# A dynamic convolution feeding a maxout layer: the start's sums, one unit's transpose and the last stores rearranged

## The chip, the core and the metric

The kernel runs on one core of a Trainium2 chip. The metric is device time in microseconds (us), from the start of the program to its end; lower is better. Times of whole runs are medians over several runs. A profile is one execution, and its span runs from the first instruction recorded to the last.

The engines are named as in the profile: PE is TensorE (PEld its weight loads), DVE is VectorE, ACT is ScalarE, POOL is GpSimd, SP is SyncE. Each works through its own queue in order.

## What is computed

```python
# x [8, 4160, 192], weight_gen [8, 4160, 8 heads, 7 taps]
w   = softmax(weight_gen, axis=-1)                     # over the 7 taps
y[b, s, h*24+g] = sum_k w[b, s, h, k] * x_pad[b, s + k, h*24+g]   # causal: x_pad has 6 zero rows ahead
# then, on y as [33280, 192], with w1, w2 [192, 1024] and w_out [1024, 192]
out = maximum(y @ w1, y @ w2) @ w_out
```

Inputs and output are float32; the kernel works in bfloat16 where it multiplies.

## The kernel before

**Layout.** The 33280 rows are laid over 128 partitions, 260 consecutive rows ("columns" in the code) to each. Columns come in batches of 16 (16 batches, and a 17th of 4). A batch is cut into pieces and a piece gives a unit: batches 0 and 1 have four pieces of 4 columns each (units 0 to 7), later ones two of 8 (units 8 to 35), and the last is unit 36 with 4. TensorE's unit of work is a tile, one per column, 260 in all: a tile is one 128-wide chunk of the 1024 hidden features for 8 columns, or two chunks for 4 columns.

**The convolution.** For a batch, `exp_sum` (L127, ACT) takes the exponentials, `red` (L132, DVE) sums them over the taps, `ln` (L135, ACT) takes the logarithm, `shift` (L140, DVE) subtracts it from the raw weights, and `weights` (L148, ACT) takes the exponential again, which is the softmax, written twice over in bfloat16. `mul` (L157, DVE) multiplies all seven taps of a piece into `m_t`. `adds` sums the taps in three instructions: L172 (taps 3, 4, 5 onto 0, 1, 2, which leaves the four slices 0, 1, 2 and 6), L177 and L179 (into `y_t`); with `first=True` only L172 is issued.

**Transposing.** From unit 8 on, `transpose` (L188) moves `y_t` through the DMA crossbar, issued on SP; a small copy on POOL, the gate (L194), waits for it, and the next loads of `x` and `weight_gen`, issued on POOL too, stand behind that gate. Units 0 to 7 go through `sum_transpose` (L215) instead: TensorE multiplies slices of `m_t` with an identity and so sums the remaining taps and transposes at once, into PSUM; ACT copies the result out (L220). Units 0 to 3 have all seven taps summed on TensorE, units 4 to 7 four of them.

**The maxout.** Since max(h1, h2) = h1 + relu(h2 - h1), `hid_tile` (L247, PE) multiplies with the difference w2 - w1 (`wd`), `relu` (L257, ACT) clips it, and the output is y (w1 w_out) (L299, in `out_first`) plus the clipped part times w_out (L287), both into PSUM. `evac` (L343, ACT) copies results to `o_t` and issues the stores on ACT (L353). The small product w1 w_out (`w10`) is made at the start: `w1_transposed` (L542) transposes w1 on TensorE in 16 pieces, eight of 128 rows and eight of 64, ACT copies them to `w1t` (L548), `w10_product` (L587) multiplies.

**Order.** The schedule is written out by hand: each engine runs its instructions in the order in which the code issues them. Tiles are worked in groups: eight of two tiles (tiles 0 to 15), then groups of three, and a last one of one tile. `hidden(g, now, between, beside)` issues for a group the hidden matmuls of all tiles but the last, the first part of the results of the columns `now` (`out_first`), relus, the last tile, then the second part of the results and their evacuation. ACT relays a signal between the two parts (`relay`, L320). `extra(t)` issues the convolution of later batches: two pieces per 16 tiles, with `red`, `shift`, `ln`, `exp_sum` and `weights` of the batches after them between. Groups 0 to 3 and what lies around them are written line by line (L551 to L614); `rest_of_1` and `early` (L620 to L636) do so for groups 4 to 7.

**Buffers.** In groups 0 to 7 PSUM has two hidden tiles (`hd`) and two of tag `op`, which results, sum-transposes, w1's transposes and the w10 product share. After that there are "ab" for the first two tiles of a group, "c" for the third and a single one, "r", for results. `rest_of_results` (L426) finishes the last 8 columns in three parts, in "r", "ab" and "c". There are two buffers each for `xb_t`, `en_t` and `y_t`, and six for `yt`.

Of the kernel before, what the change touches and what calls it, by code (L numbers as in the profile page):

```python
# [17 lines left out]
def _sub(base: bass.AP, off: int, dims):  # L18
    ap = [list(base.ap[0])] + [[int(s), int(c)] for s, c in dims]
    return dataclasses.replace(base, offset=base.offset + off, ap=ap)  # L20
# [3 lines left out]
def kernel(  # L24
# [9 lines left out]
    nc = tc.nc  # L34
# [90 lines left out]
    def exp_sum(b):  # L125
        e_ts[b] = pe_.tile([P, BATCHES[b][1] * WGC], FP32, name="e_t", tag="e")
        nc.scalar.activation(out=e_ts[b], in_=wg_ts[b], func=AF.Exp)  # L127

    def red(b):
        TH = BATCHES[b][1] * H  # L130
        s_ts[b] = psm.tile([P, TH], FP32, name="sum_t", tag="sum")
        nc.vector.reduce_sum(out=s_ts[b], in_=_sub(e_ts.pop(b), 0, [[K, TH], [1, K]]), axis=AX.X)  # L132

    def ln(b):
        nc.scalar.activation(out=s_ts[b], in_=s_ts[b], func=AF.Ln)  # L135
# [7 lines left out]
    def weights(b, o):  # L143

        N = dict(pieces(b))[o] * H
        if b not in en_ts:
            en_ts[b] = pen.tile([P, 16 * WGC * 2], BF16, name="en_t", tag="en")
        nc.scalar.activation(  # L148
            out=_sub(en_ts[b], o * WGC * 2, [[2 * N, K], [2, N], [1, 2]]),
            in_=_sub(wg_ts[b], o * WGC, [[1, K], [K, N], [0, 2]]), func=AF.Exp,  # L150
        )


    def mul(b, o):

        n = dict(pieces(b))[o]
        nc.vector.tensor_tensor(  # L157
            out=m_t[:, K * o * D:K * (o + n) * D],
            in0=_sub(xb_ts[b], o * D, [[D, K], [1, n * D]]),
            in1=_sub(en_ts[b], o * WGC * 2, [[2, K * n * H], [0, G // 2], [1, 2]]),  # L160
            op=ALU.mult,
        )
# [40 lines left out]
    def half(j):  # L203
        return slice(64 * j, 64 * j + 64)

    def sum_transpose(u, taps=range(K)):

        b, o, n = UNITS[u]
        nb = n // 2 * 3
        yps = ps["r" if "r" in ps else "o"].tile([P, 1024], FP32, name="yps", tag="op")  # L210
        for k in range(nb):
            for t in taps:
                for j in range(2):
                    at = (K * o + t * n + k // 3 + j * n // 2) * D + k % 3 * 64
                    nc.tensor.matmul(  # L215
                        yps[half(j), k * P:(k + 1) * P], lhsT=m_t[:, at:at + 64],
                        rhs=ident, start=(t == taps[0]), stop=(t == taps[-1]), skip_group_check=True,
                    )
        yt = pyt.tile([P, 8 // 2 * 3 * P], BF16, name="yt", tag="yt")
        nc.scalar.copy(out=yt[:, 0:nb * P], in_=yps[:, 0:nb * P])  # L220
        yt_ts[u] = yt
# [46 lines left out]
    def place(p):  # L268

        u, i, _ = column(2 * p)  # L270
        b, o, n = UNITS[u]
        return BATCHES[b][0] + o + i, n // 2
# [36 lines left out]
    def out_second(now, go):  # L309

        for c in now[::2]:
            for f in range(FCH):
                for j in range(2):
                    mm = out_hidden(c + 1 - j, f, j)
                    if c == now[0] and f == 0:
                        tc.add_manual_dep(mm.ins, go.ins.name, SYNC, reason="bank of the other half")
# [8 lines left out]
    def evac(p, n):  # L325

        tile_, at = op_at[p]
        o = o_t[0]
        if p == NT // 2 - 1:

            for j, copy, eng in ((0, nc.scalar.copy, nc.scalar), (1, nc.vector.tensor_copy, nc.sync)):
                c = place(p)[0] + 2 * j
                copy(out=o[:, c % 24 * D:(c % 24 + 1) * D], in_=tile_[:, at + j * 512:at + j * 512 + D])  # L333
                eng.dma_start(
                    out=bass.AP(tensor=out.tensor, offset=c * D, ap=[[CPP * D, P], [1, D]]),
                    in_=o[:, c % 24 * D:(c % 24 + 1) * D],
                )
            return
        runs = [[q for q in range(p, p + n) if column(2 * q)[0] == u]
                for u in range(column(2 * p)[0], column(2 * (p + n - 1))[0] + 1)]  # L340
        for qs in runs:
            c, h = place(qs[0])
            nc.scalar.copy(out=_sub(o, c % 24 * D, [[D, len(qs)], [h * D, 2], [1, D]]),  # L343
                           in_=_sub(tile_, at + (qs[0] - p) * D, [[D, len(qs)], [512, 2], [1, D]]))
        stores = []
        for q in range(p, p + n):
            u, i, _ = column(2 * q)
            if u < NU - 1 and i == UNITS[u][2] // 2 - 1:
                stores.append((place(q)[0] - i, 2 * (i + 1)))
            if u == NU - 1:  # L350
                stores.extend((place(q)[0] + 2 * j, 1) for j in range(2))
        for c, w in stores:
            nc.scalar.dma_start(  # L353
                out=bass.AP(tensor=out.tensor, offset=c * D, ap=[[CPP * D, P], [1, w * D]]),
                in_=o_t[0][:, c % 24 * D:(c % 24 + w) * D],
            )


# [32 lines left out]
    def out_room(now, tag=None):  # L391
        tag = tag or ("r" if "r" in ps else "o")
        w, name = {"ab": (2048, "ab"), "c": (1024, "c")}.get(tag, (1024, "op"))
        tile_ = ps[tag].tile([P, w], FP32, name="op_ps", tag=name)
        for c in now:
            op_at[c // 2] = tile_, (c - now[0]) // 2 * D

    def hidden(g, now=(), between=lambda: None, beside=lambda: None):


        t0, n = GROUPS[g]
        rd = room(g)
        for t in range(t0, t0 + n - 1):
            hid_tile(t)
        if now:
            out_room(now)
            last = out_first(now)
        if len(now) > 2:
            relu(rd, t0, n - 1)
        else:  # L410
            for t in range(t0, t0 + n - 1):
                relu(rd, t, 1)
        if now:
            go = relay(last)
        hid_tile(t0 + n - 1)
        if len(now) > 2:
            beside()
        relu(rd, t0 + n - 1, 1)
        between()
        if now:  # L420
            out_second(now, go)
            evac(now[0] // 2, len(now) // 2)
        if len(now) <= 2:
            beside()
# [25 lines left out]
    with tc.tile_pool(name="pstage", bufs=1) as pstage:  # L450
# [85 lines left out]
        def w1_transposed():  # L536

            tp = ps["o"].tile([P, 1024], FP32, name="tp", tag="op")[:, :].bitcast(BF16)
            for fi in range(FCH):
                o = fi // 4 * 1024 + fi % 4 * D  # L540
                for at, kind, nr in ((0, "E", P), (P, "T", 64)):
                    nc.tensor.matmul(  # L542
                        tp[:, o + at:o + at + nr],
                        lhsT=w1[kind][0:nr, fi * P:(fi + 1) * P],
                        rhs=ident[0:nr, 0:nr], is_transpose=True, skip_group_check=True,
                    )
            for h in range(2):
                nc.scalar.copy(out=w1t[:, 4 * h * D:4 * (h + 1) * D],  # L548
                               in_=tp[:, h * 1024:h * 1024 + 4 * D])

        warm = ps["h"].tile([P, 1024], FP32, name="warm", tag="hd")  # L551

# [15 lines left out]
        nc.scalar.copy(out=w1["T"], in_=ws["T", 0])  # L568
        w_diff(1, nc.vector.tensor_copy)
        mul(0, 8)  # L570
        sum_transpose(1)
        exp_sum(1)
        red(1)
# [1 line left out]
        ln(1)  # L575
        shift(1)
        mul(0, 12)
        w1_transposed()
        weights(1, 0)
        weights(1, 4)  # L580

        def w10_product():

# [13 lines left out]


        hidden(2)
        mul(1, 0)  # L600
        adds(1, 0, True)
        exp_sum(2)
        sum_transpose(2)
        load_x(2, 0, 16)
        load_wg(4, nc.gpsimd)
        red(2)
        mul(1, 4)
        adds(1, 4, True)
        hidden(3)
        w10_product()  # L610
        sum_transpose(3)
        weights(1, 8)
        weights(1, 12)
        ln(2)  # L614

    pout = ctx.enter_context(tc.tile_pool(name="pout", bufs=1))
    o_t.append(pout.tile([P, 24 * D], FP32, name="o_t", tag="o"))
# [2 lines left out]
    def rest_of_1():  # L620
        mul(1, 8)
        shift(2)
        adds(1, 8, True)
        mul(1, 12)
        red(3)
        adds(1, 12, True)


    none = lambda: None
    early = {  # L630
        3: (none, lambda: (exp_sum(3), rest_of_1())),
        4: (lambda: sum_transpose(4, (0, 1, 2, K - 1)), lambda: weights(2, 0)),
        5: (lambda: sum_transpose(5, (0, 1, 2, K - 1)), none),
        6: (lambda: (weights(2, 8), ln(3), sum_transpose(6, (0, 1, 2, K - 1))), lambda: load_x(3, 0, 8)),
        7: (lambda: sum_transpose(7, (0, 1, 2, K - 1)), none),
    }  # L636

    def extra(t):
# [29 lines left out]
    out_room(OUTS[3])  # L668
    go = relay(out_first(OUTS[3]))
    out_second(OUTS[3], go)  # L670
    evac(OUTS[3][0] // 2, len(OUTS[3]) // 2)
    early[3][1]()
    for g in range(4, len(GROUPS)):
# [40 lines left out]
```

## Time and profile before

| what | value |
|---|---|
| median of 11 runs | 423.01 us (421.83 to 425.58) |
| the profiled execution's own time | 422.35 us |
| its span | 420.6 us |
| PE, DVE, ACT, POOL busy | 405.1, 376.9, 359.9, 72.4 us |
| granted TensorE clock | 0.998 |
| from a unit's `mul` to that of the unit two later (a batch of 16 columns) | 23.84 us |
| PE: 16 transposes of w1 (L542) | 1.8 us for eight of 128 rows, 1.6 us for eight of 64, by the records |
| PE: one 128-column sum-transpose matmul (L215) | 220 ns on record, 48 of them start within 1.37 us |
| DVE: L172, L177, L179 of a 4-column piece | 1355, 959 and 558 ns |
| ACT: copy of a sum-transpose (L220) | 802 ns |

A row of the timeline gives the start in us from the start of the span, the duration, the engine, the line, the operation, out<-in by the program's names, shapes, and in brackets the idle time of the engine before it with what ended it. A row of the groups ends with busy time, the mean duration in ns and the idle time before. Matmul records overlap, since matmuls are pipelined: the distance between starts is what one costs in a stream. An engine name with a q (ACTq, SPq) is the issue of a DMA.

### The profile page before, as it was taken

The numbers are of one execution on the slowest core, as the hardware profiler recorded it, in microseconds if no ns is written. First come the engines' busy times: TensorE is split into PE (matmuls) and PEld (weight loads), VectorE is DVE, ScalarE is ACT, GpSimd is POOL, SyncE is SP. The second block draws the span as 40 slices with busy tenths as digits, with TensorE's granted clock in tenths as the row PEclk, the third lists the DMA queues.
The fourth block names the chain that finished last, engine by engine and source line by source line (L and its number), as shares of the span: only waits on it lengthen the run. The fifth ranks groups of instructions, "written<-read, shape, count | busy, mean of one in ns | idle before, by whom it ended". The sixth has DMA issues, their size and how long they took to land.

```text
span 420.6 us, 15949 instructions
## 1 busy us (share of the span) xinstructions
PE 405.1 (96%) x7405; PEld 327.7 (78%) x7405; DVE 376.9 (90%) x176; ACT 359.9 (86%) x416; POOL 72.4 (17%) x102
## 2 busy tenths in 40 slices
PE   7899999999999999999999999999999999999984
PEld 7789899777777777777787777777787777877784
DVE  5999999998999999999999999999999999996000
ACT  5897889999998989898999899898999899887851
POOL 1510101211220121222201212201203221310000
PEclk9999999999999999999999999999999999999999
DMA  8975547686568776865786767777795786556113
GB/s 243 258 173 151 107 66 197 151 156 95 185 139 182 196 154 168 197 165 146 181 173 125 187 151 195 179 116 195 179 187 129 125 220 99 119 157 134 77 78 115
DMA packets 60259, 65.70 MB, mean 156 GB/s; under 512 B 47617, under 2 KB 48513, under 8 KB 60192
## 3 DMA queue, kind: packets, MB, share of 16 engines
q0 software_dynamic: 8128, 24.11, 28.1%
q1 hardware_dynamic: 46448, 15.10, 21.9%
q10 hardware_dynamic: 5616, 25.46, 15.7%
q8 instruction: 58, 0.95, 0.9%
q14 instruction: 9, 0.07, 0.1%
HBM read 35.96 MB, written 25.56 MB: 146 GB/s over the span
## 4 chain that ended last, share of the span: by engine, by line
DVE 68%; PE 20%; ACT 6%; issue 3%; DMA 1%; ACTq 1%; DVEq 0%
DVE m_t L157 35%; DVE m_t L172 14%; DVE m_t L177 9%; PE op_ps L287 8%; PE hd L247 7%; ACT rd_t L257 3%; DVE sum_t L132 3%; DVE wg_t L140 3%; DVE y_t L179 3%; PE op_ps L299 2%; PE yps L215 1%; ACT o_t L343 1%; DMA wg_t<-in_weight_gen_dram 1%; PE hdp L247 1%; ACT en_t L148 1%
## 5 line engine op out<-in xcount | busy, mean ns | idle before, releaser
L257 ACT ACTIVATE rd_t<-hd 128x1024 bf16<-128x1024 f32 (+1 forms) x206 | 234.6, 1184 | 31.7 <-PE hd L247 31.3
L287 PE MATMUL op_ps<-wo,rd_t 64*128 64x192 bf16 x4160 | 210.4, 243 | 0.1
L287 PEld LDWEIGHTS <-rd_t 64*128 64x128 bf16 x4160 | 180.3, 94 | 16.1 <-ACTq L320 0.3
L247 PE MATMUL hd<-yt,wd 64*128 64x512 bf16 (+1 forms) x1584 | 187.5, 360 | 0.9 <-ACT rd_t L257 0.9
L157 DVE TENSOR_TENSOR m_t<-xb_t,en_t 128x10752 bf16<-128x10752 bf16 (+1 forms) x37 | 187.5, 5070 | 0.2 <-ACT en_t L148 0.2
L247 PEld LDWEIGHTS <-wd 64*128 64x128 bf16 x1776 | 93.2, 94 | 42.2 <-issue 2.4
L194 POOL CAST gate<-yt 128x1 f32<-128x1 bf16 x29 | 36.4, 1257 | 280.8 <-DMA yt<-y_t 280.8
L172 DVE TENSOR_TENSOR m_t<-m_t 128x4608 bf16<-128x4608 bf16 (+1 forms) x33 | 78.2, 2369 | 0.1
L343 ACT COPY o_t<-op_ps 128x384 f32<-128x384 f32 (+1 forms) x99 | 57.1, 587 | 10.9 <-PE op_ps L287 10.8
L299 PE MATMUL op_ps<-w,yt 64*128 64x192 bf16 x780 | 55.4, 243 | 4.4 <-ACT o_t L343 4.3
L299 PEld LDWEIGHTS <-yt 64*128 64x128 bf16 x780 | 38.5, 94 | 21.7 <-issue 6.7
L177 DVE TENSOR_TENSOR m_t<-m_t 128x3072 bf16<-128x3072 bf16 (+1 forms) x29 | 50.2, 1730 | 1.0
L148 ACT ACTIVATE en_t<-wg_t 128x896 bf16<-128x896 f32 (+1 forms) x37 | 34.1, 936 | 1.9 <-ACT o_t L343 0.8
L333 DVE COPY o_t<-op_ps 128x192 f32<-128x192 f32 x1 | 0.4, 358 | 31.4 <-ACT o_t L333 31.4
L179 DVE TENSOR_TENSOR y_t<-m_t 128x1536 bf16<-128x1536 bf16 (+1 forms) x29 | 27.4, 944 | 1.0
L115 POOL DMA_DIRECT2D xb_t<-in_x_dram x32 | 17.2, 539 | 23.7 <-DVE m_t L157 15.7
L132 DVE TENSOR_REDUCE sum_t<-e_t 128x128 f32<-128x896 f32 (+1 forms) x17 | 17.6, 1038 | 3.0 <-ACT e_t L127 3.0
L140 DVE TENSOR_TENSOR wg_t<-wg_t,sum_t 128x896 f32<-128x896 f32 (+1 forms) x17 | 17.8, 1045 | 2.4 <-ACT sum_t L135 2.4
L127 ACT ACTIVATE e_t<-wg_t 128x896 f32<-128x896 f32 (+1 forms) x17 | 15.8, 930 | 3.9 <-DMA wg_t<-in_weight_gen_dram 3.0
L215 PE MATMUL yps<-ident,m_t 128*64 128x128 bf16 x528 | 16.5, 220 | 1.3 <-DVE m_t L157 1.3
L215 PEld LDWEIGHTS <-m_t 128*64 128x64 bf16 x528 | 15.2, 110 | 2.8 <-DVE m_t L157 1.5
L257 ACT ACTIVATE rd_t<-hdp 128x1024 bf16<-128x1024 f32 x16 | 15.8, 1032 | 1.2 <-PE hdp L247 1.2
(45 smaller groups left out, 86.8 us busy)
## 6 DMA issues: line engine op xcount, KB each, us to landing
out_dram<-o_t ACTq DMA_DIRECT2D x28, 768.0 KB, 4.5
xb_t<-in_x_dram POOLq DMA_DIRECT2D x28, 384.0 KB, 5.1
wg_t<-in_weight_gen_dram POOLq DMA_DIRECT2D x14, 448.0 KB, 6.5
xb_t<-xb_t POOLq DMA_DIRECT2D x16, 288.0 KB, 5.3
out_dram<-o_t ACTq DMA_DIRECT2D x8, 384.0 KB, 3.1
wg_t<-in_weight_gen_dram SPq DMA_DIRECT2D x2, 448.0 KB, 5.3
xs<-in_x_dram SPq DMA_DIRECT2D x2, 384.0 KB, 6.6
xb_t<-in_x_dram POOLq DMA_DIRECT2D x1, 768.0 KB, 8.0
```

Of the source, the lines that this page charges most:

```text
L148: nc.scalar.activation(out=_sub(en_ts[b], o * WGC * 2, [[2 * N, K], [2, N], [1, 2]]), in_=_sub(wg_ts[b], o * WGC, [[1, K], [K, N], [0, 2]] ...
L157: nc.vector.tensor_tensor(out=m_t[:, K * o * D:K * (o + n) * D], in0=_sub(xb_ts[b], o * D, [[D, K], [1, n * D]]), in1=_sub(en_ts[b], o * W ...
L172: nc.vector.tensor_tensor(out=taps(0, 1, 3), in0=taps(0, 1, 3), in1=taps(3, 1, 3), op=ALU.add)
L177: nc.vector.tensor_tensor(out=taps(0, 2, 2), in0=taps(0, 2, 2), in1=taps(1, 5, 2), op=ALU.add)
L179: nc.vector.tensor_tensor(out=_sub(y_ts[b], o * D, [[64, 2], [P, 3 * w // 2], [1, 64]]), in0=taps(0, 1, 1), in1=taps(2, 1, 1), op=ALU.add,)
L194: nc.gpsimd.tensor_copy(out=gate, in_=yt[:, 0:1])
L215: nc.tensor.matmul(yps[half(j), k * P:(k + 1) * P], lhsT=m_t[:, at:at + 64], rhs=ident, start=(t == taps[0]), stop=(t == taps[-1]), skip_g ...
L247: nc.tensor.matmul(hid_out(t, f, j), lhsT=wd[half(j), s * F + f * P:s * F + (f + 1) * P], rhs=_sub(yt_ts[u][half(j), :], (s + j) % 3 * P, ...
L257: nc.scalar.activation(out=rd[:, k * 1024:(k + n) * 1024], in_=hd[:, at:at + n * 1024], func=AF.Relu)
L287: return nc.tensor.matmul(op_out(c), lhsT=rd[half(r), k * 1024 + at:k * 1024 + at + P], rhs=wo[half(r), f * D:(f + 1) * D], start=False, s ...
L299: nc.tensor.matmul(op_out(c + j), lhsT=yt_ts[u][half(j), (3 * i + (s + j) % 3) * P:(3 * i + (s + j) % 3 + 1) * P], rhs=w10[half(j), s * D: ...
L343: nc.scalar.copy(out=_sub(o, c % 24 * D, [[D, len(qs)], [h * D, 2], [1, D]]), in_=_sub(tile_, at + (qs[0] - p) * D, [[D, len(qs)], [512, 2 ...
```

## The change

Five things are rearranged; the arithmetic stays the same.

- `w1_transposed` issues the eight pieces of 128 rows first and then the eight of 64, and no longer copies the result: the two copies to `w1t`, and `weights(1, 0)` and `weights(1, 4)` after them, are issued behind `hidden(2)`.
- Columns 8 to 11 (unit 2): L172 is issued on VectorE behind `mul(0, 8)`, ahead of `red(1)`, and the sum-transpose takes four taps in place of seven.
- Softmax steps move: `exp_sum(2)` and `red(2)` behind `w10_product` and `mul(1, 4)`; `ln(2)` behind the second part of the first results; `exp_sum(3)` and `red(3)` behind group 4, ahead of `weights(2, 0)`.
- Columns 28 to 31 (unit 7): all three adds are issued on VectorE (behind `red(3)`), and `transpose(7)` moves the result through the crossbar, issued behind group 6, in place of the sum-transpose in group 7. Its gate on POOL comes ahead of `load_x(3, 0, 8)`.
- The last results: the group of a single tile, the last one, writes its results to "ab" in place of "r". For the last unit, the two stores of the pair before the last, on ACT, become one two-piece store on SP.

```diff
+    LEFT = (0, 1, 2, K - 1)
...
         for q in range(p, p + n):
             u, i, _ = column(2 * q)
             if u < NU - 1 and i == UNITS[u][2] // 2 - 1:
-                stores.append((place(q)[0] - i, 2 * (i + 1)))
+                stores.append((nc.scalar, place(q)[0] - i, [1, 2 * (i + 1) * D]))
             if u == NU - 1:
-                stores.extend((place(q)[0] + 2 * j, 1) for j in range(2))
-        for c, w in stores:
-            nc.scalar.dma_start(
-                out=bass.AP(tensor=out.tensor, offset=c * D, ap=[[CPP * D, P], [1, w * D]]),
-                in_=o_t[0][:, c % 24 * D:(c % 24 + w) * D],
+                stores.append((nc.sync, place(q)[0], [2 * D, 2], [1, D]))
+        for eng, c, *ap in stores:
+            eng.dma_start(
+                out=bass.AP(tensor=out.tensor, offset=c * D, ap=[[CPP * D, P], *ap]),
+                in_=_sub(o_t[0], c % 24 * D, ap),
             )
...
         if now:
-            out_room(now)
+            out_room(now, "ab" if n == 1 and "ab" in ps else None)
             last = out_first(now)
...
-            for fi in range(FCH):
-                o = fi // 4 * 1024 + fi % 4 * D
-                for at, kind, nr in ((0, "E", P), (P, "T", 64)):
+            for at, kind, nr in ((0, "E", P), (P, "T", 64)):
+                for fi in range(FCH):
+                    o = fi // 4 * 1024 + fi % 4 * D
                     nc.tensor.matmul(
...
-            for h in range(2):
-                nc.scalar.copy(out=w1t[:, 4 * h * D:4 * (h + 1) * D],
-                               in_=tp[:, h * 1024:h * 1024 + 4 * D])
+            return tp
...
         mul(0, 8)
+        adds(0, 8, True)
         sum_transpose(1)
         exp_sum(1)
         red(1)
...
         mul(0, 12)
-        w1_transposed()
-        weights(1, 0)
-        weights(1, 4)
+        tp = w1_transposed()
...
         hidden(2)
+        for h in range(2):
+            nc.scalar.copy(out=w1t[:, 4 * h * D:4 * (h + 1) * D], in_=tp[:, h * 1024:h * 1024 + 4 * D])
+        weights(1, 0)
+        weights(1, 4)
         mul(1, 0)
         adds(1, 0, True)
-        exp_sum(2)
-        sum_transpose(2)
+        sum_transpose(2, LEFT)
         load_x(2, 0, 16)
         load_wg(4, nc.gpsimd)
-        red(2)
         mul(1, 4)
-        adds(1, 4, True)
         hidden(3)
         w10_product()
+        exp_sum(2)
+        red(2)
+        adds(1, 4, True)
         sum_transpose(3)
         weights(1, 8)
         weights(1, 12)
-        ln(2)
...
         shift(2)
         adds(1, 8, True)
         mul(1, 12)
+
+    def end_of_1():
+        exp_sum(3)
         red(3)
-        adds(1, 12, True)
+        adds(1, 12)
...
     early = {
-        3: (none, lambda: (exp_sum(3), rest_of_1())),
-        4: (lambda: sum_transpose(4, (0, 1, 2, K - 1)), lambda: weights(2, 0)),
-        5: (lambda: sum_transpose(5, (0, 1, 2, K - 1)), none),
-        6: (lambda: (weights(2, 8), ln(3), sum_transpose(6, (0, 1, 2, K - 1))), lambda: load_x(3, 0, 8)),
-        7: (lambda: sum_transpose(7, (0, 1, 2, K - 1)), none),
+        3: (none, rest_of_1),
+        4: (lambda: sum_transpose(4, LEFT), lambda: (end_of_1(), weights(2, 0))),
+        5: (lambda: sum_transpose(5, LEFT), none),
+        6: (lambda: (weights(2, 8), ln(3), sum_transpose(6, LEFT)), lambda: (transpose(7), load_x(3, 0, 8))),
     }
...
     out_second(OUTS[3], go)
+    ln(2)
     evac(OUTS[3][0] // 2, len(OUTS[3]) // 2)
```

## The prediction

> **What bounds the kernel now.** I read the engine totals first, then the chain of work that ended last, then the timeline at each place where the chain changes engine.
>
> ```profile
> PE 405.1 (96%) x7405; PEld 327.7 (78%) x7405; DVE 376.9 (90%) x176; ACT 359.9 (86%) x416; POOL 72.4 (17%) x102
> DVE 68%; PE 20%; ACT 6%; issue 3%; DMA 1%; ACTq 1%; DVEq 0%
> ```
>
> By busy share TensorE (PE) is the bound, by the chain VectorE (DVE). Both are right, in different stretches. Start of one `mul` to the start of the same one a batch of 16 columns later is 23.84 us on VectorE (107.90, 131.74, 155.58), with hardly a gap. TensorE's groups have a shortest cycle of 8.59 us for 6 tiles (379.73, 388.32, 396.90), so 22.9 us for 16. VectorE is slower by about 0.9 us a batch; it starts with a lead, and TensorE eats that lead. The chain shows where it is gone:
>
> ```profile
> 22.98 0.32 ACT L135 ACTIVATE sum_t<-sum_t 128x128 f32<-128x128 f32 x1
> 23.34 1.09 DVE L140 TENSOR_TENSOR wg_t<-wg_t,sum_t 128x896 f32<-128x896 f32 x1 [0.87 <-ACT sum_t L135]
> ...
> 101.56 1.09 DVE L140 TENSOR_TENSOR wg_t<-wg_t,sum_t 128x896 f32<-128x896 f32 x1 [1.13 <-ACT sum_t L135]
> ...
> 283.75 0.21 POOL L194 CAST gate<-yt 128x1 f32<-128x1 bf16 x1 [14.18 <-DMA yt<-y_t]
> ...
> 352.30 0.23 ACT L135 ACTIVATE sum_t<-sum_t 128x32 f32<-128x32 f32 x1 [0.58 <-DVE sum_t L132]
> 352.44 1.00 ACT L257 ACTIVATE rd_t<-hd 128x1024 bf16<-128x1024 f32 x1
> 353.34 0.79 ACT L343 COPY o_t<-op_ps 128x768 f32<-128x768 f32 x1
> 354.18 0.42 PE L299 MATMUL op_ps<-w,yt 64*128 64x192 bf16 x6 [0.35 <-ACT o_t L343]
> ```
>
> After 12 us VectorE idles for more than a fraction of a microsecond only twice (0.87 and 1.13 us), both times for a logarithm on ScalarE (ACT). At 101.56 ScalarE, paced by TensorE, is the late one. At 352.30 it is the other way round: ScalarE's in-order queue stands 0.58 us on a sum from VectorE, then the relu, the evacuation and TensorE follow at once. From there TensorE runs to the end. So **the time is set by VectorE from 101.56 to 352.27, and by TensorE after it**. A microsecond that TensorE saves before 283 us is worth nothing unless VectorE also comes earlier; one that it saves at the end counts in full. The tail holds such waste:
>
> ```profile
> 405.56 0.42 PE L299 MATMUL op_ps<-w,yt 64*128 64x192 bf16 x6 [0.95 <-ACT o_t L343]
> 408.78 0.42 PE L299 MATMUL op_ps<-w,yt 64*128 64x192 bf16 x6 [0.82 <-ACT o_t L343]
> 414.61 0.48 ACT L343 COPY o_t<-op_ps 128x384 f32<-128x384 f32 x1 [0.77 <-PE op_ps L287]
> 415.11 1.49 ACTq L353 DMA_DIRECT2D out_dram<-o_t  x2
> 416.64 0.32 ACT L333 COPY o_t<-op_ps 128x192 f32<-128x192 f32 x1 [1.56 <-issue]
> 417.05 0.36 DVE L333 COPY o_t<-op_ps 128x192 f32<-128x192 f32 x1 [31.41 <-ACT o_t L333]
> 417.43 0.36 SPq L334 DMA_DIRECT2D out_dram<-o_t  x1
> ```
>
> TensorE waits twice for the one results bank to be evacuated, and the last evacuation waits 1.56 us while ScalarE issues two stores.
>
> [...]the 16 transposes of w1, alternating 128 and 64 rows, start 0.145 us apart, the warm-up matmuls of one shape 0.067 us apart (115 in 7.71). [...]halved operands cost more than half: the trace has 0.96 us for 128x1536 against 1.76 for 128x3072.
>
> **Part by part.** The sum is made on the profiled execution (span 420.6, time 422.35, 0.7 under the median of 423.01) and its change carried to the median.
>
> *w1's transposes.* 16 matmuls took 2.23 us (20.94 to 23.17). In two blocks, 8 at 0.067, 8 at about that or less[...] make some 1.1: about 1.1 us less. Bounds: nothing, and 1.6. But the next tile needs the hidden bank that ScalarE's second relu leaves at 22.1, and its second half the one left at 23.1, so 0.7 us at most is felt.
>
> *Four taps for columns 8 to 11.* 36 matmuls fewer at 0.0285 us (48 in 1.37): 1.0 us off TensorE. On VectorE one add of 128x2304 comes in, 1.28 us from start to next start (30.20 to 31.48), ahead of red(1).
>
> *What that does to ScalarE.* ln(1) waits for red(1), which now ends at 22.67 + 1.08 = 23.75 instead of 22.47; queued behind ln(1) are the relus of the third group, then the two w1t copies and weights(1,0), (1,4). ln starts at 23.78, and VectorE's shift at 24.12 (0.34 after, as at 7.08 and 7.42) instead of 23.34. **VectorE is 0.78 us later**, because 0.5 of the old 0.87 idle is used. ScalarE: 0.8 later by ln, then 0.84 earlier because exp_sum(2) goes behind the w10 copies: these end at about 32.4, as before (32.52). So the first outputs start at best 0.4 earlier, and the relay behind them stands after exp_sum(2), yt(3) and two weights, at about 35.0, as before (35.05). **TensorE's 2 us saved here are lost to ScalarE's order.** weights(1,0) ends at about 28.0, and VectorE wants it at 28.0: I add 0.05 for that wait (bounds: 0 and 0.5). red(2) and ln(2) have over 1 us of room where they now stand.
>
> *Columns 28 to 31.* Off TensorE: 48 matmuls, 1.46 us (52.26 to 53.72), and off ScalarE one copy of 0.80. The next group takes the old hidden banks, free after the relu at 53.4, so TensorE gains 0.95 to 1.46. On VectorE the second and third add come in; from the last batch's own such block (382.69, 384.08, 385.08), the three take 1.39 + 1.00 + about 0.48 from start to start against 1.27 for the one alone: **1.60 us**. exp_sum(3), moved behind the evacuation of group 4, delays its relus by under 1 us, and TensorE has its sum-transposes to do meanwhile: nothing (at most 0.5). The crossbar move takes 4 us (385.76 to 389.76 for this size), lands near 53.5 and is read near 70: hidden. SP's queue is empty then. POOL's gate waits for it, and load_x(3,0,8) and its halo copy are behind that gate: 54 instead of 45, for a product at 83; hidden.
>
> *VectorE's sum.* 0.78 + 0.05 + 1.60 = 2.4 us later at the first big product (47.00). At 101.56 ScalarE's logarithm comes no later than before (TensorE being some 1.2 earlier), so the 1.13 of idle goes: **2.4 − 1.1 = +1.3 us** from there to the end of VectorE's work. Bounds 0.9 and 1.8.
>
> *The 1.2 us that TensorE gains early* shrink the lead by 2.5 with VectorE's 1.3. Taking each transpose's last landing from its semaphore, that lead at the unit's first hidden matmul was 12.4 us at unit 8, 7.0 at 17, 3.1 at 23, 0.04 at 26 (283.63 for 283.67), 0.7 at 30, 1.4 at 33, 2.6 at 35. So TensorE meets VectorE some batches earlier, waits, and leaves the logarithm at 352.3 exactly as much later as VectorE is: +1.3.
>
> *The tail.* With the results of the one-tile group in the large bank (free since the relu that ends at 402.74), the first L299 follows the matmuls at 404.4 instead of 405.56: 1.1 us. The next part's bank is then free since 405.5, so it starts straight after the 0.7 us of matmuls from 407.01, at 407.75 instead of 408.78: 1.0. Part two needs the large bank evacuated by 408.4 (shifted); that copy ends near 407.7. The two stores leave ScalarE (0.974 and 0.472 of issue), so the last evacuation starts 0.28 after TensorE's end at 415.23, not at 416.64: 1.1. The SP store takes their place; its two-piece shape is not in the trace. It is issued near 413.0 and takes 0.34 to 0.97, the last store behind it being ready at 414.2: nothing, at worst 0.3. **Tail: −3.2 us**, bounds 2.1 and 3.5.
>
> *Sum:* +1.3 − 3.2 = −1.9. Span 418.7, and for the median 423.0 − 1.9 = **421.1**.
>
> **Rivals.**
> (A) TensorE is the bound and the lead suffices: then its early 1.2 us count, and VectorE's 1.3 don't: 423.0 − 1.2 − 3.2 = 418.6. For it: 96% busy, and no matmul of the page waits for yt. Against: 0.04 us of lead at unit 26 and the wait at 352.30.
> (B) The tail gives only its two bank waits (2.1), because the SP store holds up the last one, and weights(1,0) comes 0.5 late: +1.8 − 2.1, so 422.7. For it: the unseen store, the zero margin at 28.0. Against: the store has 1.2 us.
> (C) Slower: TensorE now runs pressed against the landings, and a late crossbar move near the end has nothing after it to absorb it. Landings take 3.6 to 6.8 us from issue, but unit 26's took 8.72. At unit 32 the allowance from issue (346.43) to use (353.00) is 6.57; 8.72 there costs 2.15: 421.1 + 2.15 = 423.25, slower than before. It decides from a landing of about 8.5 us. For it: one of 29 did so. Against: only units 32 to 35 count.
>
> **How the numbers follow.** The forecast has 0.58 (own range 420.2 to 421.9), A 0.17, B 0.15, C 0.10. A measurement of this kernel can tell about 0.3%, 1.27 us, from no change, so faster means under 421.7. Faster: 0.51 of the forecast, 0.17 of A, 0.02 of B, together 0.70. Same: 0.07, 0.12 of B, 0.05 of C: 0.24. Slower: 0.05 of C (two late landings), 0.01 of B: 0.06. The range goes from 418.5, under A, to 422.6, which leaves out C and half of B.
>
> **What would show it.** Right: the first L157 of 128x10752 at about 49.4; no idle before L140 near 102; the waits of L135 for L132 on ScalarE in several batches instead of one; TensorE waiting for yt or ScalarE from about 200 us; no stall of L299 at the end; the last store issued some 1.9 us earlier. Wrong: the lead at unit 35 above 2 us would mean A; ScalarE issuing nothing but the last copy late, C or B. If VectorE's mul(1,0) starts later than 28.1, the early order is mispriced.

## The result and the profile after

| | before | changed |
|---|---|---|
| median | 423.77 us (50 runs, 421.83 to 426.54) | 420.40 us (13 runs, 420.03 to 428.3) |
| ratio of the two | | 0.9922 [0.9903, 0.9942] |
| profiled execution, its span | 422.35, 420.6 us | 420.4, 418.6 us |
| PE, DVE, ACT busy | 405.1, 376.9, 359.9 us | 402.1, 379.6, 359.0 us |

The kernel is **3.3 us faster** by the ratio (0.78% of 423.77), its time 0.7 under the forecast of 421.1 and inside the range. Runs more than 1.5% above the fastest of their kernel (one of the changed kernel's 13, at 428.3; without it its median is 420.38) are left out of the ratios, and of the medians and ranges of the experiments below. The two profiled executions differ by less: 2.0 us, where the sum said 1.9. So two things are to be explained: where the 2.0 came from, and why the medians show 1.4 more.

The engine totals of the changed kernel, and its chain of waits by engine:

```profile
PE 402.1 (96%) x7321; PEld 326.2 (78%) x7321; DVE 379.6 (91%) x179; ACT 359.0 (86%) x415; POOL 71.5 (17%) x103
DVE 61%; PE 25%; DMA 5%; issue 4%; ACT 3%; SPq 1%; DVEq 0%
```

VectorE did 2.7 us more, TensorE 3.0 less, and the chain still runs mostly over VectorE. DMA has gone from 1% to 5%: that is new.

**The early part.** In the timeline of the changed kernel (start, duration, engine, line, operation, tiles, idle time before with what ended it; rows picked out), at the second softmax, at columns 28 to 31 and at the fifth batch's `shift`:

```profile
22.64 1.08 DVE L132 TENSOR_REDUCE sum_t<-e_t 128x128 f32<-128x896 f32 x1
23.75 0.31 ACT L135 ACTIVATE sum_t<-sum_t 128x128 f32<-128x128 f32 x1 [0.79 <-DVE sum_t L132]
24.09 1.09 DVE L140 TENSOR_TENSOR wg_t<-wg_t,sum_t 128x896 f32<-128x896 f32 x1 [0.38 <-ACT sum_t L135]
...
46.36 1.35 DVE L172 TENSOR_TENSOR m_t<-m_t 128x2304 bf16<-128x2304 bf16 x1
47.74 0.96 DVE L177 TENSOR_TENSOR m_t<-m_t 128x1536 bf16<-128x1536 bf16 x1
48.73 0.56 DVE L179 TENSOR_TENSOR y_t<-m_t 128x768 bf16<-128x768 bf16 x1
49.21 5.75 DVE L157 TENSOR_TENSOR m_t<-xb_t,en_t 128x10752 bf16<-128x10752 bf16 x1
...
102.56 1.08 DVE L140 TENSOR_TENSOR wg_t<-wg_t,sum_t 128x896 f32<-128x896 f32 x1
```

ScalarE now waits 0.79 us for the sum, as forecast, and the shift starts at 24.09 (23.34 before, +0.75). The first big product starts at 49.21 (47.00 before, +2.21). At 102.56 there is no bracket: the 1.13 us of idle are gone, and VectorE is 1.00 us behind the kernel before. From there it stays so: the crossbar issue of unit 35 moves from 379.93 to 380.93.

**The late part.** The piece of the chain where it leaves VectorE for good, in order of time (start, us, what). A row of DMA lasts from a transfer's issue to its landing; the first one here lands at 311.68 + 7.44 = 319.12, and the matmuls that waited for it start at 319.16:

```profile
310.58 0.97 DVE y_t L179
311.68 7.44 DMA yt<-y_t
319.16 0.82 PE hd L250 x6
...
323.59 7.99 DMA yt<-y_t
331.72 1.47 PE hd L250 x12
```

TensorE ran into two crossbar landings (7.44 and 7.99 us after issue, units 29 and 30), and its groups came 1.09 us later to the end: tile 256 starts at 400.42 instead of 399.33. The waits view of the changed kernel (us in total, times, longest) has one row that has grown and one that the kernel before lacks:

```profile
ACT sum_t L135 <- DVE sum_t L132: 5.3, 4, 1.9
...
PE hd L250 <- DMA yt<-y_t: 1.1, 2, 0.8
```

ScalarE's wait for VectorE has grown from 1.7 us in two to 5.3 in four. Both are VectorE being the late one.

**The tail**, in the timeline of the changed kernel (rows picked out):

```profile
405.52 0.43 PE L302 MATMUL op_ps<-w,yt 64*128 64x192 bf16 x6
407.74 0.43 PE L302 MATMUL op_ps<-w,yt 64*128 64x192 bf16 x6
413.56 0.48 ACT L346 COPY o_t<-op_ps 128x384 f32<-128x384 f32 x1 [0.77 <-PE op_ps L290]
414.07 0.41 SPq L356 DMA_DIRECT2D out_dram<-o_t  x1
414.23 0.32 ACT L336 COPY o_t<-op_ps 128x192 f32<-128x192 f32 x1 [0.18 <-PE op_ps L290]
415.02 0.34 SPq L337 DMA_DIRECT2D out_dram<-o_t  x1
```

Neither L302 waits for a bank now, and the last evacuation waits 0.18 us instead of 1.56. The sum of the profile: TensorE +1.09; the pair's evacuation at 413.56 instead of 414.61, so the bank gave 1.09 + 1.05 = 2.14; the last evacuation at 414.23 instead of 416.64, so the stores gave 2.41 - 1.05 = 1.36; and from the last store's issue to the end of the span 3.58 instead of 3.17, so 0.41 is given back. 1.09 - 2.14 - 1.36 + 0.41 = **-2.0**.

### The profile page after: what moved, and what is told of

The parts are those of the page before. It is cut to its first block, busy times and chain, and to the rows that moved or that the text cites. A ratio compares the mean times of both kernels' runs of the same rounds, so it can differ in the third digit from the quotient of the medians.

```text
span 418.6 us, 15794 instructions
## 1 busy us (share of the span) xinstructions
PE 402.1 (96%) x7321; PEld 326.2 (78%) x7321; DVE 379.6 (91%) x179; ACT 359.0 (86%) x415; POOL 71.5 (17%) x103
## 4 chain that ended last, share of the span: by engine, by line
DVE 61%; PE 25%; DMA 5%; issue 4%; ACT 3%; SPq 1%; DVEq 0%
DVE m_t L157 31%; DVE m_t L172 12%; PE op_ps L290 12%; PE hd L250 9%; DVE m_t L177 9%; DMA yt<-y_t 4%; DVE y_t L179 3%; DVE sum_t L132 3%; DVE wg_t L140 3%; PE op_ps L302 2%; DMA ws1T<-in_moe_w_dram 2%; ACT rd_t L260 1%; PE yps L218 1%; PE hdp L250 1%; ACT en_t L148 0%
## 5 line engine op out<-in xcount | busy, mean ns | idle before, releaser
L172 DVE TENSOR_TENSOR m_t<-m_t 128x4608 bf16<-128x4608 bf16 (+1 forms) x34 | 79.5, 2339 | 0.1
L302 PE MATMUL op_ps<-w,yt 64*128 64x192 bf16 x780 | 55.4, 243 | 4.6 <-ACT o_t L346 3.9
L302 PEld LDWEIGHTS <-yt 64*128 64x128 bf16 x780 | 38.7, 94 | 21.6 <-issue 7.2
L177 DVE TENSOR_TENSOR m_t<-m_t 128x3072 bf16<-128x3072 bf16 (+1 forms) x30 | 51.1, 1704 | 1.0
L218 PE MATMUL yps<-ident,m_t 128*64 128x128 bf16 x444 | 13.7, 220 | 0.6 <-DVE m_t L157 0.5
L218 PEld LDWEIGHTS <-m_t 128*64 128x64 bf16 x444 | 12.7, 110 | 2.0 <-issue 0.9
```

The source lines that it names most:

```text
L172: nc.vector.tensor_tensor(out=taps(0, 1, 3), in0=taps(0, 1, 3), in1=taps(3, 1, 3), op=ALU.add)
L177: nc.vector.tensor_tensor(out=taps(0, 2, 2), in0=taps(0, 2, 2), in1=taps(1, 5, 2), op=ALU.add)
L218: nc.tensor.matmul(yps[half(j), k * P:(k + 1) * P], lhsT=m_t[:, at:at + 64], rhs=ident, start=(t == taps[0]), stop=(t == taps[-1]), skip_g ...
L302: nc.tensor.matmul(op_out(c + j), lhsT=yt_ts[u][half(j), (3 * i + (s + j) % 3) * P:(3 * i + (s + j) % 3 + 1) * P], rhs=w10[half(j), s * D: ...
```

## The experiments

The kernel before ran beside each group of kernels, with medians of 423.94 to 424.39. Where a time stands against the changed kernel, it is against 420.40.

| kernel | median, us | runs, from to | ratio to before | span of the profile |
|---|---|---|---|---|
| tail alone | 421.14 | 22, 419.70 to 423.18 | 0.9936 [0.9917, 0.9956] | 420.8 |
| all but the tail | 422.89 | 22, 422.36 to 427.32 | 0.9986 [0.9967, 1.0006] | 423.0 |
| changed, unit 7 as before | **418.61** | 6, 418.16 to 420.6 | 0.9883 [0.9849, 0.9918] | 416.4 |
| the same, unit 2 as before too | 421.31 | 22, 419.37 to 425.3 | 0.9942 [0.9918, 0.9966] | 418.6 |
| tail alone, TensorE +2 us | 423.42 | 22, 421.2 to 425.74 | 0.9993 [0.9973, 1.0014] | 421.2 |
| changed, TensorE +2 us | 422.52 | 11, 420.23 to 426.50 | 0.9983 [0.9948, 1.0018] | 418.2 |
| changed, VectorE +1 us | 421.45 | 21, 421.07 to 426.20 | 0.995 [0.9927, 0.9973] | 419.9 |
| changed, old stores | 420.62 | 10, 420.35 to 423.47 | 0.9931 [0.9905, 0.9958] | 419.0 |
| changed, old bank | 422.2 | 12, 421.97 to 422.59 | 0.9956 [0.9935, 0.9976] | 420.6 |
| changed, w1 alternating | 420.87 | 7, 420.18 to 421.74 | 0.9922 [0.9891, 0.9952] | 418.3 |
| unit 7 as before, 45 matmuls added at unit 2 | 420.95 | 7, 420.49 to 422.63 | 0.9929 [0.9899, 0.9958] | 419.4 |
| tail alone, 45 matmuls added at unit 2 | 421.86 | 16, 420.15 to 424.14 | 0.9946 [0.9924, 0.9967] | 422.4 |

### The tail alone, and all but the tail

The kernel before with the bank and the stores of the change, and the changed kernel without them:

```diff
-            out_room(now)
+            out_room(now, "ab" if n == 1 and "ab" in ps else None)
...
+                stores.append((nc.sync, place(q)[0], [2 * D, 2], [1, D]))
```

> The kernel before with the last part of the change alone: the one-tile group's results in the large bank, and the two last-but-one stores as one on SP. If VectorE sets the time in the middle (my theory), the early part of the change costs 1.0 us and this kernel is the faster of the two: span 417.5, 3.1 below before and 1.1 below the changed kernel. If TensorE is the bound throughout (rival A), the early part is worth 1.7 us, this kernel still takes 3.1 off before, and the changed kernel would have had to be at 415.9, which it is not; so A can only hold if this tail gives far less, about 0.3 us, span 420.3.

> The changed kernel without the last part: results of the one-tile group in the old bank, the stores on ScalarE. Theory: VectorE is 1.0 us later at the end, so span 421.6, 1.0 above before, although TensorE does some 84 matmuls less. Rival A (TensorE bound): 1.7 us less than before, 418.9.

Measured: the tail alone gives 2.8 us (421.14 against 423.94), the rest alone 1.1, with an interval that still holds no change. Neither went as expected. The rest alone was to lose 1.0; by itself it speaks for rival A, which had it gain 1.7. The tail alone was expected to beat the changed kernel and is 0.7 slower than it. Its lowest run, 419.70, does beat the changed kernel's lowest, 420.03; its median does not. The profile of the tail alone shows why a median can stand so far above the lowest run. At TensorE:

```profile
29.21 0.94 PE L247 MATMUL hdp<-yt,wd 64*128 64x256 bf16 x14 [1.61 <-issue]
...
35.95 0.51 PE L287 MATMUL op_ps<-wo,rd_t 64*128 64x192 bf16 x8 [1.23 <-issue]
```

and at VectorE:

```profile
103.96 1.09 DVE L140 TENSOR_TENSOR wg_t<-wg_t,sum_t 128x896 f32<-128x896 f32 x1 [1.65 <-ACT sum_t L135]
```

TensorE stood 1.61 and 1.23 us in the middle of a row of equal matmuls, waiting for no engine and no transfer that the profile names ("issue"). ScalarE then is late, and VectorE idles for ScalarE twice (1.60 us at 66.47, and here), so the shift starts at 103.96, 2.40 later than in the kernel before. A further 0.8 us of this execution lies at its very end: its last store took 3.10 us to land, that of the changed kernel's profile 2.30. The profile of before has one such stall too, of 0.38 us:

```profile
28.17 0.94 PE L247 MATMUL hdp<-yt,wd 64*128 64x256 bf16 x14 [0.38 <-issue]
```

The rest alone had a crossbar landing of 10.32 us for unit 30 in its profiled execution, so its span of 423.0 says little; most of its runs lie within 422.36 and 423.05.

### Unit 7 as before, and unit 2 too

```diff
-        adds(1, 12)
+        adds(1, 12, True)
...
-        6: (..., lambda: (transpose(7), load_x(3, 0, 8))),
+        6: (..., lambda: load_x(3, 0, 8)),
+        7: (lambda: sum_transpose(7, LEFT), none),
```

The second one also takes back the four taps of columns 8 to 11:

```diff
         mul(0, 8)
-        adds(0, 8, True)
...
-        sum_transpose(2, LEFT)
+        sum_transpose(2)
```

> The changed kernel with columns 28 to 31 as before: only the first add on VectorE, four taps and the transpose on TensorE, no crossbar move of unit 7. Theory: VectorE has 1.6 us less to do, TensorE 1.5 us more; VectorE's shift at 102.56 comes some 1.3 us earlier (then held by ScalarE's logarithm at about 101.2), so span 417.3, 1.3 below the changed kernel. Rival A: 1.0 to 1.5 us slower than the changed kernel, 419.6 to 420.1.

> As e3, and columns 8 to 11 with seven taps on TensorE as well, with no add on VectorE: what is left of the change are the order of the steps, w1's transposes by row count and the last part. Theory: another 1.3 us off VectorE early, but the logarithm near 101 stands in its way, so little or nothing more than e3: span 417.0 to 417.6. Rival A: 1.0 us slower than e3, 420.6 to 421.

Measured: unit 7 back on TensorE gives **418.61, 1.8 us under the changed kernel**, the best of all. TensorE has 48 matmuls more and VectorE two adds less: VectorE is what counts. 1.3 was expected, since the logarithm was thought to hold VectorE again; it did not. The shift of the fifth batch starts without a wait, 2.19 earlier than in the changed kernel:

```profile
100.37 1.08 DVE L140 TENSOR_TENSOR wg_t<-wg_t,sum_t 128x896 f32<-128x896 f32 x1
```

Of the 2.19, 0.61 is already there at the second shift (23.48 for 24.09), which leaves 1.58 for the two adds, priced at 1.60.

Unit 2 back as well was expected to be faster again or equal, and is 2.7 us slower, though VectorE has one add less. Its profile shows stalls of the kind seen in the tail alone (0.66 us at 22.43 and the one below), and later an idle time on VectorE. TensorE:

```profile
28.35 0.94 PE L250 MATMUL hdp<-yt,wd 64*128 64x256 bf16 x14 [0.89 <-issue]
```

VectorE, in the same kernel:

```profile
101.70 1.09 DVE L140 TENSOR_TENSOR wg_t<-wg_t,sum_t 128x896 f32<-128x896 f32 x1 [0.99 <-ACT sum_t L135]
```

So the 36 matmuls that the change takes from TensorE at unit 2 are worth something after all, and at the median more than their 1.0 us. Not all of the difference is theirs for certain: of the 2.2 us between the two profiles (418.6, 416.4), 1.33 are in the shift (101.70 for 100.37), and 0.8 are in the landing of the last store, 3.14 us after its issue for 2.31.

### A load on TensorE, a load on VectorE

70 more matmuls (1.98 us from 44.77 to the next at 46.75, in the profile of the tail alone with them) in the sum-transpose of unit 5, into a bank half that the real ones write afterwards, once in the tail alone and once in the changed kernel:

```diff
+        if u == 5:
+            for i in range(70):
+                nc.tensor.matmul(yps[half(i % 2), 0:P], lhsT=m_t[:, K * o * D:K * o * D + 64],
+                                 rhs=ident, start=True, stop=True, skip_group_check=True)
```

and in the changed kernel the sum of batch 3 made twice over:

```diff
...
+        if b == 3:
+            nc.vector.reduce_sum(out=s_ts[b], in_=_sub(e_ts[b], 0, [[K, TH], [1, K]]), axis=AX.X)
```

> The tail-only kernel with 70 more matmuls (about 2.0 us of TensorE) ahead of unit 5's sum-transpose, near 42 us; they write what is written over after. My theory of the wide spread of the tail-only kernel: in it (as before the change) the logarithm near 101 us holds VectorE, so whatever TensorE loses in the first 100 us lengthens the run one for one. Then 421.1 becomes about 423.1. If VectorE alone set the time from the start, nothing would change.

> The changed kernel with the same 70 matmuls. There the logarithm is done 2.7 us before VectorE wants it, so 2.0 us lost on TensorE disappear: 420.4 to 420.7. Rival A (TensorE bound throughout): 422.4.

> The changed kernel with batch 3's sum over the taps done twice on VectorE (1.0 us more). Theory, VectorE bound: 1.0 us slower one for one, 421.4. Rival A: no change.

Measured: in the tail alone 2 us on TensorE cost 2.3 at the median; in its profile the shift waits for ScalarE's logarithm again (idle 1.65) and starts at 105.12, 1.16 later than in the profile of the tail alone. One more microsecond on VectorE cost the changed kernel 1.1, as expected of an engine that sets the time. The load on TensorE in the changed kernel is half an answer: the profiled execution, at 420.26, absorbed the 2 us wholly (span 418.2, no idle on VectorE after 24 us), but the median is 2.1 above the changed kernel, where rival A had it, and the runs spread from 420.23 to 426.50. None of the longer ones was profiled, so **what makes them longer stays open**.

### The two halves of the tail, and the order of w1

```diff
-            out_room(now, "ab" if n == 1 and "ab" in ps else None)
+            out_room(now)
```

```diff
-            for at, kind, nr in ((0, "E", P), (P, "T", 64)):
-                for fi in range(FCH):
+            for fi in range(FCH):
+                for at, kind, nr in ((0, "E", P), (P, "T", 64)):
```

For the old stores the code of the kernel before is put back, two stores issued on ScalarE.

> The changed kernel with the two last-but-one stores back on ScalarE as two. Step of the sum: the last evacuation waits for their issue again, 1.1 us slower, 421.5. If the store's engine doesn't matter: 420.4.

> The changed kernel with the one-tile group's results back in the bank that the group before has to evacuate first. Step of the sum: two waits of TensorE come back, 2.1 us slower, 422.5. If the waits are hidden anyway: 420.4.

> The changed kernel with w1's transposes alternating between 128 and 64 rows as before. TensorE has about 1.2 us more to do near 22 us. Theory: ScalarE's order hides it, 420.4 to 420.7. Rival A: 421.6.

Measured: the bank is worth 1.8 us, and its two waits return as they were (0.95 and 0.82 us), so the term of 2.1 stands within 0.3:

```profile
406.48 0.42 PE L302 MATMUL op_ps<-w,yt 64*128 64x192 bf16 x6 [0.95 <-ACT o_t L346]
...
409.70 0.42 PE L302 MATMUL op_ps<-w,yt 64*128 64x192 bf16 x6 [0.82 <-ACT o_t L346]
```

The stores are worth 0.2, not 1.1. With the old ones in the changed kernel:

```profile
414.19 1.00 ACTq L356 DMA_DIRECT2D out_dram<-o_t  x2
415.24 0.32 ACT L336 COPY o_t<-op_ps 128x192 f32<-128x192 f32 x1 [1.07 <-PE op_ps L290]
...
416.03 0.35 SPq L337 DMA_DIRECT2D out_dram<-o_t  x1
```

The two issues took 1.00 us here (0.974 and 0.472 in the kernel before, 1.00 again in the kernel without the tail), so the last store is issued 1.01 later, 0.13 of which came before the tail. But it landed 1.68 us after its issue, and 2.30 in the changed kernel, where the two-piece store left 0.95 us ahead of it on the same queue. Of the 0.88 that the issue gains, the landing gives 0.62 back. The DMA views of the kernel before and of the changed one show the last store so (KB, median us from issue to landing):

```profile
out_dram<-o_t SPq DMA_DIRECT2D x1, 96.0 KB, 1.8
...
out_dram<-o_t SPq DMA_DIRECT2D x1, 96.0 KB, 2.3
```

The other profiles agree: it lands 1.7 to 1.8 us after its issue in the three with the old stores, 2.3 in eight with the new one, and 3.1 to 3.2 in the remaining three. Whether the shared queue makes the difference, or the time at which the stores leave, no run separates.

The order of w1's transposes is worth 0.5 at the median and 0.15 between the lowest runs (420.18, 420.03), with intervals that overlap: no difference that these runs can show.

### The mechanism of the stalls

The trace has all records of TensorE's weight loads and all DMA packets, those of the queue named "instruction" among them. The timelines of all 14 kernels have 21 rows in which TensorE waits 0.2 us or more for "issue" ahead of a matmul, all of them before 37 us. Counting loads from the start, they lie within two loads of number 224, 352, 480 or 608: 128 apart, which with a matmul to each load is 256 instructions. The page of the tail alone has, among its queues (packets, MB, share):

```profile
q8 instruction: 58, 0.95, 0.9%
```

Each packet has 16384 bytes, and with 58 of them for 2 x 7405 = 14810 of TensorE's matmuls and loads there is one to 255. What they carry, no view shows; the trace gives their times. Counted from load 224, each block of 128 loads in the kernel before and in the changed one starts after the packet of the same number has ended, to the last of the 57 and 56 blocks, and 1.34 us after it at the least. Some of them ("entered" is the first load of the block before):

| kernel, first load of block | entered | packet | first load starts | after packet's end |
|---|---|---|---|---|
| before, 352 | 16.09 | 19.33 to 20.27 | 21.98 | 1.71 |
| before, 480 | 21.98 | 25.73 to 26.71 | 28.17, stalled | 1.45 |
| before, 608 | 28.17 | 31.10 to 32.08 | 33.54 | 1.47 |
| tail alone, 480 | 21.79 | 26.97 to 27.85 | 29.21, stalled | 1.36 |
| tail alone, 608 | 29.21 | 33.49 to 34.38 | 35.95, stalled | 1.57 |
| changed, 352 | 15.95 | 19.62 to 20.60 | 21.94, stalled | 1.34 |
| changed, 480 | 21.94 | 26.03 to 26.99 | 29.16 | 2.17 |
| changed, 608 | 29.16 | 29.29 to 30.51 | 34.53 | 4.03 |

In these 14 profiles none of the blocks that begin with loads 224 to 736 starts sooner than 1.25 us after its packet ended, and the 21 stalls all end 1.25 to 1.57 us after it. So **each stall ends shortly after a packet of that queue does**. That TensorE waits there for its own instructions is the author's reading of these times; no run tests it apart. Ahead of the 21 stalls the packet starts 3.0 to 5.7 us after TensorE entered the block before, and that block lasts 5.6 to 8.0 us; where no stall follows, the packet starts 0.0 to 4.4 us after. Why it starts late in one execution and not in another stays open.

Two more kernels bear on this: 45 matmuls (90 instructions, 1.25 us from 24.30 to the next at 25.55 in the profile of the best kernel with them) added at unit 2, in the best kernel and in the tail alone, with the edit shown above for `u == 2` and 45. Their expectations speak of TensorE's time alone.

> The kernel with unit 7 as before (e3) and 45 more matmuls (1.3 us of TensorE) ahead of unit 2's sum-transpose, near 24 us. In e3 the logarithm near 101 is in time by 0.13 us only, so if e3 is steady it is because TensorE waits for ScalarE until 32 us and a loss before that is absorbed: 418.6 to 418.9. If the loss passes on: 419.9.

> The tail-only kernel with the same 45 matmuls near 24 us. There TensorE doesn't wait for ScalarE before 32 us, and what it loses goes on to the logarithm near 101: 421.1 becomes about 422.2 (1.0 to 1.3 slower). If it is absorbed as in e3: 421.1.

Measured: the best kernel lost 2.3 us, far more than expected of it, and its profile has a stall at load 480 that it did not have, with VectorE idle later:

```profile
28.64 1.47 PE L254 MATMUL hdp<-yt,wd 64*128 64x256 bf16 x23 [1.32 <-issue]
```

```profile
102.50 1.09 DVE L140 TENSOR_TENSOR wg_t<-wg_t,sum_t 128x896 f32<-128x896 f32 x1 [1.60 <-ACT sum_t L135]
```

The shift starts 2.13 later than in the best kernel. The rest of the 3.0 us between the two profiles (419.4, 416.4) is in the landing of the last store, 3.21 us after its issue for 2.31.

The tail alone lost 0.7 at the median, within its spread; its profiled execution is its slowest, with the largest stall of all, after a packet that started 5.72 us after the block before was entered:

```profile
29.74 1.17 PE L219 MATMUL yps<-ident,m_t 128*64 128x128 bf16 x35 [2.48 <-issue]
```

The added matmuls move other work onto these places (L219 stalls at loads 480 and 608, where in the tail alone it was L247 and L287), and the stalls stayed at the count. No run changed the number of instructions and left TensorE's work as it was, so what a stall adds to a whole run is read from the profiles, not tested by itself.

## Why the prediction was right, and where it was wrong

**VectorE sets the time to 352 us: right.** A microsecond on VectorE cost 1.1, two adds taken off it gave 1.8 though TensorE had 48 matmuls more. Rival A, TensorE as the bound throughout, falls with these two. It has two medians on its side all the same: the rest alone gained 1.1, and 2 us on TensorE in the changed kernel cost 2.1. So what holds in the profiled executions is not the whole account of the usual run.

**The number: partly luck.** The forecast of 421.1 carried -1.9 to a median of 423.0. The later median before is 423.77, and from there -1.9 gives 421.9, 1.5 over what was measured. The sum was right for the profiled executions (-2.0), with VectorE's part and the stores' part each a little smaller than said.

**VectorE's sum: +1.3 said, +1.00 measured.** The logarithm cost 0.75 (0.78 said), the first big product came 2.21 later (2.4 said), and the idle of 1.13 went wholly. The difference is in the early terms of 0.78 and 1.60 and in the start, which itself varies by tenths between executions; the last 0.3 isn't split further.

**Unit 7's move: priced right, and a loss.** The text had it at 1.60 on VectorE against a gain on TensorE that VectorE would not let through. The experiment gives 1.8.

**"TensorE meets VectorE some batches earlier, waits": right, with one thing added.** The lead at a unit's first hidden matmul was 0.96 us at unit 18, 0.40 at 28 and 0.04 at 29. There it was the crossbar's landing, not only the logarithm, that held TensorE. That is rival C's mechanism, three units before the stretch that it named; TensorE came out 1.09 late, with VectorE, and not 2.15.

**The bank: 2.1 said, 2.14 in the profile, 1.8 by experiment.** Right.

**The stores: the term that was mis-sized.** 1.1 said; 1.36 in issue less 0.41 after it by the two profiles, 0.2 by experiment. Two things failed in it. It took the issue's 0.974 and 0.472 from one execution, where two others had 1.00 for both. And it let the time end with the last store's issue, when what ends it is that store's landing (at 419.27 and 417.32; the span ends 1.30 later in both profiles). Rival B, which gave the stores nothing, was nearer in size, but had its doubt in the wrong place: the SP queue was not late (414.07 for a last store at 415.02); the landing was.

**"TensorE's 2 us saved here are lost to ScalarE's order": right for the profiled execution, wrong for the median.** This step failed. In the profile of the kernel before, TensorE followed the packets closely up to 33.54 us: loads 480 and 608 started 1.45 and 1.47 us after theirs, and the stall of 0.38 at 28.17 stood in the timeline. The idle of 1.13 on VectorE at 101.56, for which the text held ScalarE "paced by TensorE" to account, had this stall behind it for a part, and in other executions, as in the profile of the tail alone, longer ones. The change takes 72 instructions out of that stretch and makes TensorE wait for ScalarE at 27.32 (0.56 us) and 32.26 (0.70) anyway. In its profile loads 480 and 608 start 2.17 and 4.03 us after their packets, so by the least of the 14 profiles, 1.25, 0.9 us and more are to spare, and the logarithm of the fifth batch is done 2.7 us before VectorE wants it; in the kernel before VectorE waited 1.13 for it. The spare time is what counts, not that no stall can come: the changed kernel with the old bank, the same program up to its end, stalled at load 608, and VectorE had no idle for it (shift at 102.46):

```profile
36.05 1.25 PE L290 MATMUL op_ps<-wo,rd_t 64*128 64x192 bf16 x26 [1.23 <-issue]
```

On a good execution this is worth nothing, as far as single lowest runs can tell: lowest against lowest, the early part costs 0.3 (420.03 for 419.70) beside the tail and 0.8 without it (422.36 for 421.57). On a usual one it gains: 0.7 beside the tail, 1.1 without, both with intervals that overlap. That is where the medians' 1.4 beyond the profiles come from, as far as the profiled executions tell; a run without a profile shows no packets, so for those it is inferred. The last store's landing, 0.8 us longer in three of eleven profiles with the new store, is a second source of spread, and how much each has in the medians is not known.

**w1's order: right that little of it is felt, for another reason.** The text gave the hidden banks as the limit. Load 352 lies among these transposes in either order, and starts at 21.98 before and 21.94 after, 1.71 and 1.34 us after its packet ended (20.27 and 20.60):

```profile
21.93 0.27 PE L545 MATMUL tp<-ident,w1E 128*128 128x128 bf16 x2 [0.63 <-issue]
```

From the first transpose to the first matmul behind them, about 1.5 us pass in the changed kernel (20.79 to 22.30) instead of 2.2 (20.94 to 23.17). The transposes start 0.15 us apart in the alternating order; in the grouped one the first six of 128 rows start 0.06 apart, the eight of 64 0.03. But 0.63 of the 1.5 are that wait, which takes back a part of what the grouped order saves. Behind it, TensorE waits 0.56 us for ScalarE's copy to `w1t` at 27.32.

**Left open:** why 2 us on TensorE cost the changed kernel 2.1 at the median and nothing in its profile; what of the medians' 1.4 is in stalls on "issue" and what in the last landing; why a crossbar landing takes 7.44, 7.99 or 10.32 us in one execution and not in the next.

**The better kernel** is the changed one with unit 7 as before: the tail and the early four taps are kept, and VectorE isn't asked for two more adds. It runs in 418.61 us (six runs), 0.9883 [0.9849, 0.9918] of the kernel before.

## What to carry to other kernels

Before moving work between engines, find the engine whose microseconds count by loading and unloading it. Here the trade settled what busy shares (96% for TensorE) could not: with 48 matmuls more on TensorE and two adds less on VectorE the kernel ran 1.8 us faster. Look at the profile and the median both, since they can disagree, as they did for 2 us on TensorE. A store at the end was worth what its landing gained, not what its issue gained: here 0.2 us, by experiment, where the issue gained 0.88. And where a tightly packed stretch shows short stalls on "issue" that come back at the same instruction counts, count instructions as well as their durations: there the 36 matmuls, of 1.0 us, were worth 2.7 at the median, of which the profiles tie 1.3 to VectorE coming earlier.

## What the runs showed that was not expected

- Up to about 37 us TensorE stood on "issue" 21 times in 14 profiles, for 0.2 to 2.5 us, at places 128 loads apart and 1.25 to 1.57 us after a packet of the queue "instruction" had ended; the block before such a stall lasted 5.6 to 8.0 us.
- Two stores issued on ScalarE took 1.00 us in two executions and 1.45 in another.
- The last store landed 2.3 us after its issue in eight executions and 3.1 to 3.2 in three, behind a two-piece store on its own queue, and 1.7 to 1.8 in the three where that data left from ScalarE's.
- Crossbar landings of the same size took up to 10.32 us.
